# A fused delta-rule attention and MLP kernel: a new hand-written order for steps two to four, the substitution and the weight conversions of its opening

## Chip, cores and metric

The kernel runs on one core of one Trainium2 chip. The metric is device microseconds (us) for the whole kernel, lower being better. Before the change the median of three runs is 663.7 us (661.84 to 664.44).

## What is computed

The first half is a recurrent delta rule over 768 tokens, for 4 batches and 8 heads of width 48. The second half is an MLP with a hardswish on the 3072 rows that result.

```python
def _attn_ref(q, k, v, beta):
    k_n = k / (np.linalg.norm(k, axis=-1, keepdims=True) + 1e-06)
    for t in range(S):
        y[:, :, t] = np.einsum('bhd,bhde->bhe', q[:, :, t], state)
        v_old = np.einsum('bhde,bhd->bhe', state, kt)
        state = state + bt[:, :, :, None] * np.einsum('bhd,bhe->bhde', kt, vt - v_old)
def _moe_ref(x, w_in, w_out):          # x: 3072 x 384, d_ff 2048
    h = x @ w_in
    g = h * np.clip(h + 3.0, 0.0, 6.0) / 6.0
    return (g @ w_out).astype(np.float32)
```

The two weight matrices arrive as 64-bit floats. The kernel converts them to fp32 on the chip.

## The kernel before

**Tiling.** The tokens are cut into 24 steps of 32 tokens. One step holds all four batches (4 x 32 = 128 partitions) and all heads. Within a step the recurrence becomes a triangular system, whose inverse X is needed; across steps a state is carried. Two steps make one block of 256 rows for the MLP. The steps are grouped for the inversion: step 0 alone is group 0, steps 1 to 4 are group 1, and so on by fours.

**Order.** The instructions of each engine run in the order in which the program issues them. For steps 0 to 4 and the first MLP block that order is a text, `ORDER` (L22 to L41): each word advances one generator by one piece (`do`, L1428), and `*3` says it three times. From step 5 on a planner in the code takes over (L1469). Python generators fix only the order of issue, so every wait follows from data and buffers.

**Words that matter here**, with the number of the step or group behind the letter:

- `k`, `q`, `v`, `w`: one DMA issue on SyncE (SP) each. Keys, queries and values come in four parts per step; `w` is a 768 KB piece of weights, 16 in all (`load_w`, L320). A piece 6 or later reuses the buffer of an earlier one.
- `a`: one of four ScalarE instructions per weight piece, which build the power of two of each weight (`scales`, L345, instruction at L356). In this text a7.2 is the third of the four for piece 7, counting from zero. They write one of two buffers in turn, so a8.0 waits until the last conversion of piece 6 has read its buffer (L352).
- `c`: one of three VectorE instructions per piece, which convert the weights (`convert`, L366; L378, L383, L389). c6.2 is the last one of piece 6, and it needs a6.3.
- `n4`: norms of the keys of step 4 (`norms`, L399): a square and a root on ScalarE, the rest on VectorE.
- `p4`: preparation of step 4 (`prep`, L505), seven pieces: scaled keys on GpSimd; TensorE transposes of keys; a ScalarE copy; transposes of queries; a copy; scores on TensorE (L547); two VectorE products (L558) that mask the scores.
- `m`, `b`: the mask and the beta-scaled keys on GpSimd (L486, L498). `z` and `s`: settings.
- `x0`: the inverse of step 0 by products (`product`, L569).
- `i1`: the inverses of steps 1 to 4 together (`halves_of`, L715), 31 VectorE pieces: a transposition (L469), 28 small products and subtractions by turns (L730, L735), a memset, and a transposition back (L473). The first needs the masked scores of all four steps. It leaves the inverse of the two diagonal halves of each triangle.
- `x1`: the joining of the halves for step 1 (`join`, L666): a memset, a VectorE transposition (L694), a TensorE product (L684), a VectorE sum and transposition (L698, L702), a second product (L684), a ScalarE copy (L710).
- `h1`: the chain of step 1 (`chain`, L787): the product with the state on TensorE (L806), R on VectorE (L901, L909), the product with X (L827), its copy Z on ScalarE (L927), the product for the state (L938), the new state on VectorE (L956). Step 0 has no state yet and begins with the product with X.
- `y1`: the output of step 1 (`output`, L837), six pieces: a ScalarE copy (L843), a VectorE sum (L819), a TensorE product with Z (py, L827), a VectorE sum, the transposes (yt, L873), and a ScalarE copy into the MLP's input xT (L877). `y0` has four: py, copy, yt, copy.
- `ua`, `ra`, `ga`: one column block of the up product for step 0's rows: six matmuls (L994), the ScalarE relu (L1001), the VectorE rest (L1004). There are 16 column blocks; each pair needs one converted weight piece. `ub`, `rb`, `gb` do the same for step 1's rows.

**Buffers.** Results of TensorE go to four rotating slots (`pm`, L144) for everything named above but the scores and states, which share two (`pc`). The scores of a step free their slot when both masked products have read them; the first state product `h0` needs both slots.

The words ORDER holds just before the stretch that the change touches end in

```
n4 k p1 k p2*2 x0*2 a*2 c a*2 q*3
a*2 w v p3*2
```

so at its start step 0's inverse lacks one piece, keys of steps 2 and 3 are on their way through TensorE, weight pieces 0 to 2 are converted and the scalings of piece 3 are done.

Of the kernel before, what the change touches and what calls it, by code (L numbers as in the profile page):

```python
# [22 lines left out]
k*2 B*3 k*2 n0 k*2 z B s*2 n0*6 k*2 q*2 n1 q n1 q w k p0 z*3 k n1*2 k*2 n1*2 z p0*2 s k p0*3 a k a  # L23
m0 a n2 m1 p0 x0*2 w q x0 n1 x0*3 c*2 n2 a k s p1*2 a s*2 k q s*2 x0 n2 k*2 c x0 n2 x0 w q a*4 q p1
n2 k*2 a x0 m2 p1 c*2 p1 n2*3 b1 q b0 s p1 x0 q w x0 n2 q*2 c*3 x0 n4 k p1 k p2*2 x0*2 a*2 c a*2 q*3
a*2 w v p3*2 q x0 q n4 p2*2 c p2 v c n4*2 a*3 z v n4 c a m3 v c p2 n4*2 q p2 k c b2 h0 c h0 w a*2 h0
p4*2 a*2 m4 p3 q*4 h0 q k w p4*2 c*5 v*2 p3 k p3*3 k*2 p4*2 v*2 p4 m6 k a w a w i1*3 k i1*7 a i1*2 a
i1*2 v i1*2 k b3 k y0 c y0*3 ua*2 ra*2 i1*3 w v ga v a*3 i1*2 ua i1 h1 i1 q w ua ra ua i1 ra*2 ga i1
k ua a*2 ra ga i1 ga ua ra ua ra i1 ga i1*4 ua ga n5 x1*2 k x1 c a ra v a*2 ga x2 k*2 ga*2 ua*2 x1
ra*2 x1*2 ua h1*2 n5 k ga c ra ga*2 h1 c y1*2 ua ra w ga ua ra x2 n5 ga y1*2 ua ra ga h1 v*3 n5*2 k  # L30
y1*2 ua a ra x2 ub*2 a n5 rb*2 h1 x3 ga c*2 v W a h2 y2 gb ub rb gb x2 gb ub*2 n5*2 b4 rb n5 x2*2 h2
gb rb gb m5 a n5*2 y2 ub rb gb v c q*2 v q*5 n5 ub n5 rb gb h2 c h2 q ub y2 h2 y2 rb ub p5 b5 rb
gb*2 a*2 x3 p5 ub y2*2 k p5*2 h2 rb h3 p5 gb h3 ub*2 q rb gb rb gb ub a x3 p6 v c x4 x3 rb gb ub p7
rb gb y3 c*2 v c p7*2 y3 v p7*2 b6 x3 q x3 ub p6 h3 a p6 c p5*2 rb gb k m7 w p6 h3 u p6 k*2 q*3 a*2
y3 a p6 c y3 v y3*2 u n9 v k q a c a c*2 u*2 ru gu w k a*2 c a*2 x4 c*2 ru p7 a gu k u a*2 p7 p6 m8
u*3 a k u*2 k h3 w ru*2 a*2 gu*2 x4 c*2 x4 k c*2 a p8 k a*2 u ru k h3 u*2 h4 ru a b8 gu k gu y4 p8*3
u h4 k*2 c q k*9 q u p8*2 x4 k ru k*2 gu k c n9 q u q*2 p8 k*2 b7 n9*2 i2 u x4 q i2*2 q ub ru gu u
rb gb i2*2 h4*2 u*2 i2 ru i2*6 y4 i2 gu i2*7 u i2 ru gu i2 u*3 ru i2*4 gu ru i2*2 v i2 c gu u*3 a u
ru c i2 u*2 i2 gu i2*3 q i2*5 y4 h4 n9 i2 e*2 n9*2 i2*4 q i2 y4 e n9 u ru i2*3 u i2 ru*2 gu h4 u n9
i2*2 u i2 e i2*6 y4 u k n9*3 u gu i2 y4 n9 i2 p9 q i2*2 gu  # L40
"""  # L41


# [1521 lines left out]
```

## Time and profile before

| | |
|---|---|
| median of three runs | 663.7 us |
| the profiled execution, its own time | 662.06 us |
| its span in the profile | 660.3 us |
| PE busy, share of the span | 632.5 us, 96% |
| DVE busy | 499.2 us, 76% |
| ACT busy | 282.3 us, 43% |
| POOL busy | 225.1 us, 34% |
| matmul and weight-load instructions | 11640 each |

PE is TensorE's matmul stream, PEld its weight loads, DVE VectorE, ACT ScalarE, POOL GpSimd, SP the engine that issues most DMAs. Shares over the whole span hide the stages: in the first 50 us PE is busy for little more than half of the time, later all the time. So the views used below are those of stretches of time: a table of busy time by stretch, the chain of work that ended last, and the instructions in order of time. Times in them are us from the span's start. The busy time of PE is modelled, and a busy PE is not PE at its peak. The granted clock (PEclk) is the share of full speed that TensorE was allowed.

### The profile page before, as it was taken

What the parts mean: (1) busy time and instruction counts of PE and PEld (TensorE: products, weight loads), DVE (VectorE), ACT (ScalarE), POOL (GpSimd) and SP (SyncE); (2) the same over time, 40 slices, a digit from 0 to 9 for tenths busy, and PEclk for the clock granted to TensorE, in tenths of its full rate; (3) what the DMA queues carried; (4) which work ended last, traced back from release to release, by engine and by line L of the source; (5) the groups of instructions that cost most, each with busy time, mean ns of one, the idle gap of its engine ahead of it and who ended that gap; (6) DMA issues with size and microseconds to landing.
All of it is one profiled execution on the core that took longest, in us unless ns stands there. A gap on an engine that the chain in (4) does not pass through costs nothing.

```text
span 660.3 us, 26640 instructions
## 1 busy us (share of the span) xinstructions
PE 632.5 (96%) x11640; PEld 569.2 (86%) x11640; DVE 499.2 (76%) x1170; ACT 282.3 (43%) x548; POOL 225.1 (34%) x352
## 2 busy tenths in 40 slices
PE   2768999999999999999999999999999999999997
PEld 2658987776689989999999999999999999999997
DVE  5899877798657988758988848979658998456354
ACT  5887689332243154154154244244244144153250
POOL 6531022003661353553254354164051242331430
PEclk9998999999999999999999999999999999999999
DMA  7888346202040030041030030020020020000000
GB/s 174 204 198 235 77 102 164 51 25 43 9 87 18 3 74 3 3 90 22 3 74 3 2 74 3 2 63 2 3 50 2 3 49 3 23 18 2 26 1 24
DMA packets 88692, 33.28 MB, mean 50 GB/s; under 512 B 80224, under 2 KB 83424, under 8 KB 88576
## 3 DMA queue, kind: packets, MB, share of 16 engines
q1 hardware_dynamic: 88224, 31.29, 20.8%
q8 instruction: 91, 1.49, 0.9%
q10 hardware_dynamic: 352, 0.30, 0.2%
q14 instruction: 25, 0.20, 0.1%
HBM read 26.84 MB, written 4.72 MB: 48 GB/s over the span
## 4 chain that ended last, share of the span: by engine, by line
PE 91%; DVE 3%; DMA 2%; SPq 1%; ACT 1%; issue 1%; DVEq 0%
PE po L1226 28%; PE ph L1066 27%; PE ph L994 9%; PE po L1162 6%; PE ks L806 4%; PE su L938 3%; PE pt L524 3%; PE pz L827 3%; PE py L827 3%; PE sc L547 2%; PE yt L873 1%; DMA spare<-in_moe_w_in_dram 1%; PE pi L684 1%; DMA w_out<-in_moe_w_in_dram 1%; SPq L168 1%
## 5 line engine op out<-in xcount | busy, mean ns | idle before, releaser
L1066 PE MATMUL ph<-xT,w_in 128*128 128x128 f32 (+1 forms) x720 | 156.8, 321 | 0.0
L1030 POOL TENSOR_TENSOR g<-g 128x256 f32<-128x256 f32 (+1 forms) x144 | 88.6, 616 | 104.7 <-ACT g L1080 99.1
L1066 PEld LDWEIGHTS ph<-xT,w_in 128*128 128x128 f32 x720 | 116.8, 191 | 6.7
L1226 PE MATMUL po<-w_out,g 128*128 128x192 f32 x640 | 110.6, 326 | 0.0
L1226 PEld LDWEIGHTS po<-w_out,g 128*128 128x128 f32 x640 | 104.6, 190 | 0.5
L1080 ACT ACTIVATE g<-ph 128x512 f32<-128x512 f32 x72 | 43.1, 598 | 105.1 <-PE ph L1066 105.1
L1226 PE MATMUL po<-spare,g 128*128 128x192 f32 x480 | 86.7, 332 | 0.0
L1226 PEld LDWEIGHTS po<-spare,g 128*128 128x128 f32 x480 | 77.2, 190 | 1.8
L994 PE MATMUL ph<-xT,w_in 128*128 128x128 f32 (+1 forms) x384 | 72.0, 338 | 0.6 <-ACT xT L877 0.6
L1236 POOL TENSOR_TENSOR o<-o,u 128x192 f32<-128x192 f32 x18 | 13.3, 739 | 163.8 <-ACT o L1233 86.6
L994 PEld LDWEIGHTS ph<-xT,w_in 128*128 128x128 f32 x384 | 59.6, 195 | 7.7 <-ACT xT L877 0.8
L1093 DVE TENSOR_TENSOR g<-ph,g 128x256 f32<-128x256 f32 x72 | 30.2, 419 | 46.8 <-PE ph L1066 33.5
L759 DVE TENSOR_TENSOR pr<-A 128x30 f32<-128x30 f32 (+9 forms) x150 | 57.3, 382 | 3.3
L1212 DVE TENSOR_TENSOR g<-g 128x512 f32<-128x512 f32 x80 | 56.1, 722 | 3.5 <-PE po L1226 3.5
L1113 DVE SCALAR_TENSOR_TENSOR g<-o,g 128x512 f32<-128x512 f32 x72 | 52.6, 730 | 7.8 <-ACT o L1110 7.7
L764 DVE TENSOR_TENSOR A<-A,pr 128x30 f32<-128x30 f32 (+9 forms) x150 | 55.1, 367 | 3.3
L1110 ACT ACTIVATE o<-g,halves 128x512 f32<-128x512 f32 x72 | 52.2, 725 | 11.3 <-DVE g L1113 8.4
L1066 PE MATMUL ph<-beta_tok,sums_in 128*128 128x128 f32 x288 | 55.9, 275 | 0.0
L356 ACT ACTIVATE spare<-spare,places 128x768 uint16<-128x768 uint16 (+1 forms) x56 | 52.8, 947 | 3.2 <-DMA kf<-in_k_dram 1.6
L1233 ACT ACTIVATE o<-po 128x192 f32<-128x192 f32 x40 | 13.3, 332 | 82.7 <-PE po L1226 79.2
L510 POOL TENSOR_TENSOR kb<-kf,inv 128x384 f32<-128x384 f32 x24 | 21.7, 907 | 75.5 <-issue 43.1
L1162 PE MATMUL po<-w_out,g 128*128 128x384 f32 x128 | 45.4, 490 | 0.0
(141 smaller groups left out, 1019.1 us busy)
## 6 DMA issues: line engine op xcount, KB each, us to landing
kf<-in_k_dram SPq DMA_DIRECT2D x96, 48.0 KB, 2.6
qb<-in_q_dram SPq DMA_DIRECT2D x96, 48.0 KB, 2.4
vf<-in_v_dram SPq DMA_DIRECT2D x96, 48.0 KB, 2.1
out_dram<-o SPq DMA_DIRECT2D x90, 48.0 KB, 1.6
spare<-in_moe_w_in_dram SPq DMA_DIRECT2D x4, 768.0 KB, 6.6
w_out<-in_moe_w_in_dram SPq DMA_DIRECT2D x4, 768.0 KB, 6.1
w_out<-in_moe_w_out_dram SPq DMA_DIRECT2D x4, 768.0 KB, 5.8
spare<-in_moe_w_out_dram SPq DMA_DIRECT2D x4, 768.0 KB, 5.2
```

Source lines behind the costliest of these rows:

```text
L356: nc.scalar.activation(out=z, in_=z if n else d.bitcast(I16)[:, :, :, 3], func=func, bias=places[:, n : n + 1], scale=scale,)
L759: nc.vector.tensor_tensor(out=pv, in0=A[:, j + 1 :, j].unsqueeze(2).to_broadcast([n, w, j]), in1=A[:, j, 0:j].unsqueeze(1).to_broadcast([n ...
L764: nc.vector.tensor_tensor(out=A[:, j + 1 :, 0:j], in0=A[:, j + 1 :, 0:j], in1=pv, op=ALU.subtract)
L994: nc.tensor.matmul(ph[:, cols], lhsT=w_in[:, s, f * 128 : (f + 1) * 128], rhs=xT[:, s, cols], start=(s == 0), stop=(s == NKT - 1),)
L1030: nc.gpsimd.tensor_tensor(out=out, in0=a, in1=b, op=op)
L1066: nc.tensor.matmul(ph[:, n], lhsT=w, rhs=x, start=start, stop=stop, skip_group_check=True)
L1080: nc.scalar.activation(out=gt, in_=ph[:], func=ACTF.Copy)
L1110: nc.scalar.activation(out=r, in_=g, func=ACTF.Relu, bias=half, scale=1.0 / 6.0)
L1113: nc.vector.scalar_tensor_tensor(out=g, in0=r, scalar=1.0, in1=g, op0=ALU.min, op1=ALU.mult)
L1162: nc.tensor.matmul(pos[c][:], lhsT=gs[blk, f // 2][:, f % 2, c * P : (c + 1) * P], rhs=w_out[:, f, :], start=(f == 0), stop=(f == NFC - 1),)
L1212: nc.vector.tensor_tensor(out=A(f, *out, 4), in0=A(f, *a, 4), in1=A(f, *b, 4), op=op)
L1226: nc.tensor.matmul(ps[n][:], lhsT=A(f - f % 2, *a)[:, f % 2], rhs=b[:, f], start=(f == 0), stop=(f == HF - 1),)
```

## The change

Only the text `ORDER` changes. The first 148 and the last 338 of its 782 words stay as they are. The 296 between them are the same words in another order, so that every instruction of before is there once, on the same engine and of the same shape. The core of the diff, from which the unchanged words that merely wrap differently are left out (the new stretch ends at `n5 k c` in its last line):

```diff
@@ -23,21 +23,21 @@
-a*2 w v p3*2 q x0 q n4 p2*2 c p2 v c n4*2 a*3 z v n4 c a m3 v c p2 n4*2 q p2 k c b2 h0 c h0 w a*2 h0
-p4*2 a*2 m4 p3 q*4 h0 q k w p4*2 c*5 v*2 p3 k p3*3 k*2 p4*2 v*2 p4 m6 k a w a w i1*3 k i1*7 a i1*2 a
-i1*2 v i1*2 k b3 k y0 c y0*3 ua*2 ra*2 i1*3 w v ga v a*3 i1*2 ua i1 h1 i1 q w ua ra ua i1 ra*2 ga i1
-k ua a*2 ra ga i1 ga ua ra ua ra i1 ga i1*4 ua ga n5 x1*2 k x1 c a ra v a*2 ga x2 k*2 ga*2 ua*2 x1
-ra*2 x1*2 ua h1*2 n5 k ga c ra ga*2 h1 c y1*2 ua ra w ga ua ra x2 n5 ga y1*2 ua ra ga h1 v*3 n5*2 k
...
+a*2 w v p3*2 m3 b2 q n4 x0 q p2*2 n4 c p3 v*2 p3 n4 p2 n4*3 p4 c p4 p3 p2 p4 v q*3 w c p3 a p2 m4 c
+k p4 p3 p4 h0 a c p4 q*3 k w h0 p4 i1 a v*2 k*3 h0 a y0 v*2 h0 c y0 k w y0 a y0 w m6 i1*3 ua a k
+i1*3 ra ua z i1*2 a ga ra ua v i1*2 a ga ra h1 k b3 k i1*3 ga c*2 ua ra w ua ra i1*3 ga a c v ua ra
+ga i1*3 ua ra ga a v i1*3 ua ra ga i1*3 ua ra ga a q w i1*2 ua ra ga a k i1*2 ua ra ga a i1 x1*2 x2
+x1 n5 c k x1 ua ra a h1 ga x1*2 c v k*2 a h1 c a*2 c a*3 n5 k c ga h1 c y1*2 ua ra w ga ua ra x2 n5
...
```

Spelled out, with what each engine's queue sees:

- The preparation of steps 2, 3 and 4 comes first. Norms, `p3` and `p4` are interleaved from the first word on; the scores of step 4 stand before the first state product and before step 0's output, where before `h0` was complete ahead of the scores of step 3.
- The first `i1` is issued after conversions c3.0 to c4.1 (five pieces), where before c3.0 to c6.1 (eleven) stood ahead of it. c4.2, c5.0, c5.1 and c5.2 now stand inside the substitution, and c6.0 to c7.1 behind it. Before, only c6.2 stood inside, and c7.0 and c7.1 behind.
- The new state of step 0 (`h0`, last piece) and one settings piece (`z`, nine small memsets) stand inside the substitution, where before both were ahead of it.
- Step 0's output `y0` starts behind the first `i1`, where before half of the substitution was ahead of it. Eleven of the first twelve `ua` and ten `ga` stand ahead of the last `i1`; before it were eight `ua` and five `ga`.
- The scalings a4.0 to a8.3 are spread anew. The last six, a7.2 to a8.3, stand between the last piece of `x1` and the fourth piece of `h1` (Z on ScalarE). Before, all of them were ahead of that last piece of `x1`.
- On SP the last two query parts of step 4 go ahead of weight piece 5; the other loads keep nearly their places.

More of the change, by code (lines that the diff above doesn't have):

```diff
@@ L30 @@
-ra*2 x1*2 ua h1*2 n5 k ga c ra ga*2 h1 c y1*2 ua ra w ga ua ra x2 n5 ga y1*2 ua ra ga h1 v*3 n5*2 k
[L31 to L39, printed above, removed]
@@ L40 @@
-i2*2 u i2 e i2*6 y4 u k n9*3 u gu i2 y4 n9 i2 p9 q i2*2 gu
+a*2 w v p3*2 m3 b2 q n4 x0 q p2*2 n4 c p3 v*2 p3 n4 p2 n4*3 p4 c p4 p3 p2 p4 v q*3 w c p3 a p2 m4 c
[3 more added lines that the diff above has]
+x1 n5 c k x1 ua ra a h1 ga x1*2 c v k*2 a h1 c a*2 c a*3 n5 k c ga h1 c y1*2 ua ra w ga ua ra x2 n5
@@ new lines @@
+ga y1*2 ua ra ga h1 v*3 n5*2 k y1*2 ua a ra x2 ub*2 a n5 rb*2 h1 x3 ga c*2 v W a h2 y2 gb ub rb gb
+x2 gb ub*2 n5*2 b4 rb n5 x2*2 h2 gb rb gb m5 a n5*2 y2 ub rb gb v c q*2 v q*5 n5 ub n5 rb gb h2 c h2
+q ub y2 h2 y2 rb ub p5 b5 rb gb*2 a*2 x3 p5 ub y2*2 k p5*2 h2 rb h3 p5 gb h3 ub*2 q rb gb rb gb ub a
+x3 p6 v c x4 x3 rb gb ub p7 rb gb y3 c*2 v c p7*2 y3 v p7*2 b6 x3 q x3 ub p6 h3 a p6 c p5*2 rb gb k
+m7 w p6 h3 u p6 k*2 q*3 a*2 y3 a p6 c y3 v y3*2 u n9 v k q a c a c*2 u*2 ru gu w k a*2 c a*2 x4 c*2
@@ L41 @@
+ru p7 a gu k u a*2 p7 p6 m8 u*3 a k u*2 k h3 w ru*2 a*2 gu*2 x4 c*2 x4 k c*2 a p8 k a*2 u ru k h3
+u*2 h4 ru a b8 gu k gu y4 p8*3 u h4 k*2 c q k*9 q u p8*2 x4 k ru k*2 gu k c n9 q u q*2 p8 k*2 b7
+n9*2 i2 u x4 q i2*2 q ub ru gu u rb gb i2*2 h4*2 u*2 i2 ru i2*6 y4 i2 gu i2*7 u i2 ru gu i2 u*3 ru
+i2*4 gu ru i2*2 v i2 c gu u*3 a u ru c i2 u*2 i2 gu i2*3 q i2*5 y4 h4 n9 i2 e*2 n9*2 i2*4 q i2 y4 e
+n9 u ru i2*3 u i2 ru*2 gu h4 u n9 i2*2 u i2 e i2*6 y4 u k n9*3 u gu i2 y4 n9 i2 p9 q i2*2 gu
 """
```

## Prediction

> **What bounds the kernel now.** I read the table of busy time by stretch first (us from the span's start; busy us of each engine, granted clock, DMA share, GB/s).
>
> ```profile
> core 0: us, PE busy (x) PEld busy (x) DVE busy (x) ACT busy (x) POOL busy (x), PEclk, DMA share, GB/s
> 30.00:40.00 10.00, 6.33 (x245) 5.54 (x250) 8.82 (x28) 7.71 (x11) 4.79 (x5) 1.00 0.86 192
> 40.00:50.00 10.00, 6.16 (x243) 5.29 (x235) 9.25 (x15) 9.38 (x13) 3.39 (x7) 1.00 0.80 217
> 50.00:60.00 10.00, 9.42 (x120) 8.86 (x121) 9.28 (x35) 7.08 (x13) 0.20 (x2) 0.83 0.97 274
> 60.00:70.00 10.00, 9.06 (x360) 8.15 (x359) 9.41 (x26) 7.21 (x17) 2.15 (x4) 1.00 0.40 108
> 70.00:80.00 10.00, 10.00 (x311) 9.35 (x311) 8.61 (x24) 8.32 (x19) 0.00 (x0) 1.00 0.30 89
> ```
>
> From 30 to 70 VectorE (DVE) is the full engine. From about 62 on TensorE (PE) is, and the chain of waits stays with PE to the end. So what PE loses behind the substitution is not won back, and what it gains ahead of it counts only if PE is then let through. Next, that chain around the changed stretch (start, us, what).
>
> ```profile
> 45.50 0.61 DVE spare L383
> ...
> 47.79 1.86 DVE A L469
> ...
> 58.71 2.00 DVE X L473
> ...
> 60.83 0.37 DVE sums_in L694
> 61.24 0.72 PE pi L684 x54
> ...
> 67.44 0.81 PE py L827 x64
> ```
>
> Conversions run until the substitution starts (transposition A, 47.7 in the instructions in order of time). X is back at 60.7, x1's transposition ends at 61.2, py of step 1 starts at 67.4. Py is where I compare: in both orders ua13 and ua14 stand just ahead of it, and the same words behind. Last, ScalarE (ACT) in order of time.
>
> ```profile
> 58.63 1.00 ACT L356 ACTIVATE spare<-w_out,places 128x768 uint16<-128x768 int16 x1
> ...
> 61.78 1.92 ACT L356 ACTIVATE spare<-spare,places 128x768 uint16<-128x768 uint16 x2
> ...
> 64.22 0.28 ACT L710 ACTIVATE X<-pi 128x128 f32<-128x128 f32 x1
> ...
> 65.94 0.49 ACT L927 ACTIVATE R<-pz 128x384 f32<-128x384 f32 x1 [0.51 <-PE pz L827]
> 66.33 0.58 ACT L843 ACTIVATE y<-ks,parity 128x384 f32<-128x384 f32 x1
> ```
>
> The last scalings (a8.2, a8.3) end at 63.7, before X1's copy (L710) and Z1 (L927, "R"). Z1 releases py.
>
> **Part 1: scores first.** Nothing is removed; all is moved. I follow each queue from 32, where the order begins to differ, with durations of these rows. DVE: norm sum 32.0 to 32.5, x0's last piece to 33.0; root (0.3) on ACT; c3.0 (0.55); four small norm pieces (0.2 each) to 34.4. GpSimd: m3 (1.9) and b2 (0.8) end at 33.3 as before, then keys of step 4 (0.83) to 35.5. PE: their transposes (1.1) to 36.7, scores of steps 2 and 3 (1.5 for both, row at 45.2) to 38.2, query transposes to 39.2; ACT's copy (0.6, behind a4.0, 1.0) to 39.9; scores of step 4 to 41.3; the two masked products (0.75) to 42.1. A thus starts at **42.1**, 5.6 earlier. The five conversions there (0.56, 0.96, 0.95 by turns) fit beside that chain; DVE waits some 2 us in it. On SP two 0.45 us issues of queries pass weight piece 5, which lands by some 41 (6.1 us to landing) and is first read by a5.0 at about 45; that hides them. Were it not hidden, a5.0 would be late by as much, and it stands ahead of xT0. Piece 11 can be issued only after c6.1 (59 before, some 65 now); it lands in some 5 us and its scaling comes some 30 us later, so I cost it at nothing. The value loads behind it on SP are for step 3, some 20 us off.
>
> **Part 2: what now stands inside the substitution.** From A to the end of x1's transposition before took 61.2 - 47.7 = 13.5. Added: the state update 1.0, c4.2 0.95, nine memsets 0.5, c5.0 to c5.2 2.65 (42.26 to 44.91 for such three), four more `ga` at 0.2, and waits of `ga` on relus behind scalings of 0.96 on ACT, 0.5. Taken out: c6.2, 0.9. That is 5.5, so 42.1 + 13.5 + 5.5 = **61.1**. The head start is spent: the inverse comes as before. PE meanwhile starts `ua` at 46.6 in place of 51.05 (Z0 41.3, state product 43.5, py0 44.3, copy, transposes, and a copy behind a5.0 on ACT), and does eleven in place of nine blocks by then. That is the gain, at most two blocks of 0.77, or 1.5 us of PE time, and PE needs it only if it is the one waited for.
>
> **Part 3: behind the substitution.** From 61.1: first product 61.9; c6.0 (0.55) hides in that wait; sum and transposition (0.8) to 62.75; R (1.35) to 64.1; `ga` 0.2; c6.1 (1.0); c6.2 (0.95) to **66.2**. On ACT: relu 12 to 63.15, a7.1 to 64.1, X1 64.4, a7.2, a7.3 to 66.3. Now a8.0 waits for c6.2, and then a8.0 to a8.3 run (four at 0.96 to 1.0, 3.9) to 70.2. Behind them is Z1 (0.5), to 70.7, and behind Z1 the copy of y1 and relus 13 on. Py starts at 70.75, against 67.37. PE takes ua13 at 66.3 when c6.2 gives its weights, ua14 to 67.9, and then **stands for about 2.9 us**. c7.1, `ga` 12 and c7.2 end on DVE at about 69.4, just ahead of it. The sum at py is **+3.4 us**, and as PE has no wait left behind it, the same at the end.
>
> A check from DVE alone. Before, it comes through the same pieces (to the last `ga` ahead of Z1) at 66.3, with 1.8 us of waits from 32.0 on, so 32.5 of work. In the new order c7.0, c7.1, a norm sum and a `ga` (2.25) lie behind c6.2, so c6.2 ends at 32 + 30.25 = 62.25 with no wait at all, and at 65.2 with the 2.9 that I found. Then a8.x, Z1 and a gap of 0.1 make py 66.8 (-0.6) or 69.7 (+2.4). So the terms I can bound give -0.6 to about +5 (A a us later from slower cold matmuls, conversions at the 1.3 to 1.5 us that some took beside GpSimd). I take the walk, +3.4.
>
> **The clock.** [...] After 2.41 us without a matmul, 0.55 of transposes and 0.58 more, the granted clock fell:
>
> ```profile
> 51.00:52.00 1.00, 0.95 (x7) 0.95 (x8) 0.90 (x4) 0.00 (x0) 0.00 (x0) 0.90 1.17 274
> 52.00:53.00 1.00, 1.00 (x7) 1.00 (x6) 0.90 (x4) 0.37 (x1) 0.00 (x0) 0.50 1.07 258
> 54.00:55.00 1.00, 1.00 (x21) 0.78 (x22) 0.99 (x2) 0.97 (x2) 0.00 (x0) 0.50 1.01 270
> 55.00:56.00 1.00, 1.00 (x57) 0.95 (x53) 0.91 (x4) 0.97 (x2) 0.00 (x0) 0.89 0.80 136
> ```
>
> Half clock for 0.2 + 3 + 0.2 = 3.4 us. PE could spare that there, since it waited for X afterwards. Behind py it could not: half of 3.4 is 1.7 us lost. [...]
>
> **The rivals.**
> 1. *The stop also lowers the clock*: +3.4 + 1.7 = +5.1. For it, the row above; against it, that stops of 1.7 us near 39 left the clock at 1.00.
> 2. *DVE gets through with few waits*, or later waits behind py swallow part: py at -0.6 to +2.4, middle about +1. For it, the check above; against it, that the scores' chain leaves DVE idle whatever is cheap.
> 3. *Faster*: PE's early start is what counts. It decides once Z1 is ready when ua14 ends, that is if c6.2 ends by about 62 - some 4 us before my walk - or if the six scalings do not hold Z1. Then two blocks of `ua` done early are 1.5 us gained at py, and if steps 1 to 3 behind it no longer meet conversions, the 4.45 us of the earlier `ua` is the most: -1.5 to -4.5, about 660 on the medians. The conserved DVE work speaks against it.
> 4. *The change does nothing*: not possible in the order of the queues; only its sum may be near nothing, which is rival 2.
>
> **The numbers.** Against the profiled execution's own 662.06 us (span 660.3 and 1.8 around it) the forecast is 665.5. That execution lies 1.6 below the median of the runs shown, 663.7; on the median it is 663.7 + 3.4 = **667.1**. Rival 1 gives 668.8, rival 2 about 664.7, rival 3 659 to 662. Chances: forecast 0.43 (666 to 668.2), rival 1 0.25, rival 2 0.23, rival 3 0.09. The range runs from rival 2's lower half, 663.3, to rival 1 with a late A, 670.5. It leaves out rival 3 and the ends of rival 2. Half a per cent, 3.3 us, is about what a measurement of this kernel can tell from no change. Slower by more: rival 1 and about half of the forecast's own spread, 0.47. Faster by more: rival 3 where it gains over 3.3, 0.08. Within: 0.45.
>
> **What would show it.** Right: A starts near 42, X ends near 60.7, Z1 sits behind L356 rows at about 70, PE idles 2 to 3 us ahead of py at about 70.7, then shows none. The clock row behind py tells rival 1. Wrong: Z1 before 68, X before 58, or a PE that still waits or catches up between 75 and 110; or A later than 44, with more than +5.

## The result and the profile after

The changed kernel takes 670.68 us (median of 6 runs, 669.68 to 673.97); the kernel before, run beside it, 662.97 (6 runs, 661.84 to 664.44). The ratio is 1.0126, 95% interval 1.0099 to 1.0154: slower, by 7.7 us on the medians where +3.4 was forecast, and just above the upper end of the range, 670.5. The profiled execution took 670.85 us (span 669.0), 8.8 more than that of before.

First the table of busy time by stretch of the kernel after, with the columns of the prediction's first fence.

```profile
core 0: us, PE busy (x) PEld busy (x) DVE busy (x) ACT busy (x) POOL busy (x), PEclk, DMA share, GB/s
30.00:40.00 10.00, 7.11 (x260) 6.22 (x260) 8.96 (x19) 6.82 (x11) 5.43 (x6) 1.00 0.83 184
40.00:50.00 10.00, 6.59 (x214) 5.34 (x215) 6.67 (x24) 4.88 (x7) 2.26 (x5) 0.56 0.84 233
50.00:60.00 10.00, 10.00 (x124) 9.72 (x123) 7.58 (x27) 6.41 (x15) 0.00 (x0) 0.76 0.87 224
60.00:70.00 10.00, 5.84 (x208) 5.11 (x208) 9.29 (x22) 7.19 (x12) 2.86 (x4) 0.75 0.21 38
70.00:80.00 10.00, 8.60 (x218) 7.75 (x216) 6.38 (x15) 7.03 (x14) 0.00 (x0) 0.56 0.30 92
```

VectorE, the full engine of before, lost work in every stretch from 40 on: from 30 to 70 it is busy 32.5 us against 36.8. The granted clock, 0.83 in one stretch of before, is below 0.8 in four. The trace of before is no typical one in this: its mean granted clock is 0.997, and of 60 executions of that kernel on record with a clock only four reach 0.995. The 49 below 0.99 have a median of 663.16 us, the other 11 one of 662.99, so a lower mean clock does not show in the time of that kernel. Next the chain of waits from 37 to 75.

```profile
37.64 0.59 PE pt L524 x4
38.23 0.64 PE pz L827 x48
38.87 2.47 issue
41.34 0.54 PE pz L827 x16
...
61.39 1.96 DVE X L473
63.37 0.46 DVE sums_in L694
63.87 0.76 PE pi L684 x54
...
70.19 2.92 DMA vf<-in_v_dram
73.11 0.46 ACT R L927
73.61 1.50 PE py L827 x64
```

"issue" is time in which TensorE waited for nothing that the profile shows: it stood for 2.47 us in the middle of pz0, behind its 48th record. (Such a product leaves two records in the trace: pz0 is 32 products in the program and 64 records, a `ua` three and six. This text counts records.) X comes back at 63.3 (before 60.7), x1's transposition ends at 63.82 (61.19), py of step 1 starts at 73.61 (67.37). Now VectorE in order of time, only the rows with a wait and A; the bracket is the idle time and what ended it.

```profile
43.10 0.42 DVE L558 TENSOR_TENSOR L<-sc,sums_in 128x256 f32<-128x256 f32 x1 [2.90 <-PE sc L547]
...
43.78 1.95 DVE L469 STREAM_TRANSPOSE A<-L 128x1024 f32<-128x1024 f32 x1
...
51.37 0.29 DVE L1004 SCALAR_TENSOR_TENSOR g<-g,ph 128x128 f32<-128x128 f32 x1 [1.32 <-ACT g L1001]
...
52.65 0.29 DVE L1004 SCALAR_TENSOR_TENSOR g<-g,ph 128x128 f32<-128x128 f32 x1 [0.52 <-ACT g L1001]
```

A starts at 43.78 (before 47.70), behind a wait of 2.90 us for step 4's scores. Inside the substitution VectorE waits for relus: 1.32, 0.52 and, behind a third `ga`, 0.19 us. Last, ScalarE ahead of Z1 ("R", L927) in order of time.

```profile
69.27 1.02 ACT L356 ACTIVATE spare<-w_out,places 128x768 uint16<-128x768 int16 x1 [0.37 <-DVE w_in L389]
70.31 2.87 ACT L356 ACTIVATE spare<-spare,places 128x768 uint16<-128x768 uint16 x3
73.09 0.47 ACT L927 ACTIVATE R<-pz 128x384 f32<-128x384 f32 x1
```

This is the queue that the prediction spoke of: a8.0 waits for c6.2, four scalings run, then Z1. Z1 starts at 73.09 (before 65.94; forecast 70.2). The chain above puts Z1 down to a load of values that lands at 73.11 instead. But ScalarE is busy with the scalings until then, and in e1 and e7 below Z1 starts (70.98 and 69.59) within 0.5 us of the first of these loads' issue (70.55 and 69.20), and the one such load of the kernel after whose landing is known took 5.3 us. So Z1 does not wait for the load.

TensorE in order of time shows what it loses: before, then after.

```profile
51.05 3.55 PE L994 MATMUL ph<-xT,w_in 128*128 128x128 f32 x18 [0.58 <-ACT xT L877]
...
65.83 1.60 PE L994 MATMUL ph<-xT,w_in 128*128 128x128 f32 x12
...
73.20 1.15 PE L806 MATMUL ks<-state,KQ 64*64 64x48 f32 x64
```

```profile
49.29 4.21 PE L994 MATMUL ph<-xT,w_in 128*128 128x128 f32 x18 [0.58 <-ACT xT L877]
...
63.87 0.73 PE L684 MATMUL pi<-X,sums_in 16*32 16x16 f32 x64 [3.11 <-DVE sums_in L694]
...
69.28 2.93 PE L994 MATMUL ph<-xT,w_in 128*128 128x128 f32 x12 [0.58 <-DVE w_in L389]
73.61 1.50 PE L827 MATMUL py<-R,LB 32*32 32x48 f32 x64 [1.40 <-ACT R L927]
...
81.56 1.15 PE L806 MATMUL ks<-state,KQ 64*64 64x48 f32 x64
```

The last rows of both are the milestone still needed: the next state product, `ks` of step 2, starts at 81.56 (before 73.20). From there to the end it takes 587.4 us against 587.1. So all that counts is lost by then, 8.36 us, and it divides at two points:

| from, to | before | after | difference | forecast |
|---|---|---|---|---|
| start to the end of x1's transposition | 61.19 | 63.82 | +2.63 | -0.1 |
| to py | 6.18 | 9.79 | +3.61 | 3.4 to 3.5 |
| to ks of step 2 | 5.83 | 7.95 | +2.12 | 0 (rival 1: +1.7) |

### The profile page after: what moved, and what is told of

The parts are those of the page before. It is cut to its first block, busy times and chain, and to the rows that moved or that the text cites. A ratio compares the mean times of both kernels' runs of the same rounds, so it can differ in the third digit from the quotient of the medians.

```text
span 669.0 us, 26639 instructions
## 1 busy us (share of the span) xinstructions
PE 638.1 (95%) x11640; PEld 573.8 (86%) x11640; DVE 499.7 (75%) x1170; ACT 281.5 (42%) x548; POOL 224.8 (34%) x352
## 3 DMA queue, kind: packets, MB, share of 16 engines
q8 instruction: 91, 1.49, 0.9%
## 4 chain that ended last, share of the span: by engine, by line
PE 91%; DVE 3%; SPq 2%; DMA 2%; issue 1%; ACT 0%; POOL 0%; DVEq 0%; POOLq 0%
PE po L1226 28%; PE ph L1066 27%; PE ph L994 9%; PE po L1162 6%; PE ks L806 4%; PE py L827 3%; PE su L938 3%; PE pz L827 3%; PE pt L524 3%; PE sc L547 3%; PE yt L873 1%; SPq L168 1%; DMA spare<-in_moe_w_in_dram 1%; DMA w_out<-in_moe_w_in_dram 1%; PE pi L684 1%
## 5 line engine op out<-in xcount | busy, mean ns | idle before, releaser
L1066 PE MATMUL ph<-xT,w_in 128*128 128x128 f32 (+1 forms) x720 | 156.9, 321 | 0.1
L1066 PEld LDWEIGHTS ph<-xT,w_in 128*128 128x128 f32 x720 | 116.8, 191 | 6.7
L994 PE MATMUL ph<-xT,w_in 128*128 128x128 f32 (+1 forms) x384 | 74.9, 348 | 1.3 <-DVE w_in L389 0.6
L994 PEld LDWEIGHTS ph<-xT,w_in 128*128 128x128 f32 x384 | 62.3, 205 | 9.0 <-ACT xT L877 1.0
```

Source lines behind the costliest of these rows:

```text
L994: nc.tensor.matmul(ph[:, cols], lhsT=w_in[:, s, f * 128 : (f + 1) * 128], rhs=xT[:, s, cols], start=(s == 0), stop=(s == NKT - 1),)
L1066: nc.tensor.matmul(ph[:, n], lhsT=w, rhs=x, start=start, stop=stop, skip_group_check=True)
```

## The experiments

**Theory Q**: the scalings ahead of Z1 hold py, and a stop of TensorE lowers the clock. **Rival I**: the loss is the late inverse. Later, **theory F**: TensorE runs out of instructions at fixed places of its own stream. Distances: "X" is the start of the transposition back (L473), and X-py and py-ks run to the starts of py and of ks of step 2. The interval is that of the ratio to the kernel before on the same chip, whose median lies between 662.61 and 663.69 us.

| kernel | X | X-py | py-ks | median, us | ratio, 95% |
|---|---|---|---|---|---|
| before | 58.71 | 8.66 | 5.83 | 662.97 | |
| after | 61.39 | 12.22 | 7.95 | 670.68 | 1.0099 to 1.0154 |
| e1 | 63.51 | 10.75 | 8.29 | 673.22 | 1.0135 to 1.0184 |
| e2 | 57.87 | 12.71 | 7.21 | 668.08 | 1.0053 to 1.0091 |
| e3 | 61.98 | 8.68 | 5.83 | 666.58 | 1.0038 to 1.0082 |
| e4 | 60.93 | 12.50 | 7.38 | 669.88 | 1.0073 to 1.0131 |
| e5 | 63.65 | 13.71 | 5.83 | 680.95 | 1.0227 to 1.0275 |
| e6 | 61.16 | 12.54 | 5.83 | 670.11 | 1.0062 to 1.0118 |
| e7 | 62.17 | 10.74 | 7.22 | 670.37 | 1.0072 to 1.0113 |
| e8 | 61.76 | 8.74 | 7.11 | 666.98 | 1.0036 to 1.0071 |

### e2: the late scalings alone, in the kernel before

```diff
-ga v a*3 i1*2 ua i1 h1 i1 q w ua ra ua i1 ra*2 ga i1 k ua a*2 ra ga i1 ga ua ra ua ra i1 ga i1*4 ua
+ga v a*2 i1*2 ua i1 h1 i1 q w ua ra ua i1 ra*2 ga i1 k ua ra ga i1 ga ua ra ua ra i1 ga i1*4 ua
-ga n5 x1*2 k x1 c a ra v a*2 ga x2 k*2 ga*2 ua*2 x1 ra*2 x1*2 ua h1*2 n5 k ga c ra ga*2 h1 c y1*2
+ga n5 x1*2 k x1 c ra v ga x2 k*2 ga*2 ua*2 x1 ra*2 x1*2 ua h1*2 n5 k ga c ra ga*2 a*6 h1 c y1*2
```

All six, a7.2 to a8.3, go just ahead of Z1.

> The order of before, with one edit: the six scalings a7.2 to a8.3 stand just ahead of Z1 of step 1. Theory Q: ScalarE reaches them at 65.4, Z1 at about 71.2, py at 71.8 in place of 67.4 (+4.4), and a stop of some 4 us lowers the clock for 3.4 us or more (+1.7 to 2), total 667.4 to 669.5. Rival I: the inverse is as early as before, so at most 1 us slower, 663 to 664.

Measured 668.08 us, as Q expected. Its ScalarE rows and its py, from the instructions in order of time:

```profile
67.28 2.87 ACT L356 ACTIVATE spare<-spare,places 128x768 uint16<-128x768 uint16 x3
70.06 0.47 ACT L927 ACTIVATE R<-pz 128x384 f32<-128x384 f32 x1
```

```profile
70.58 0.88 PE L827 MATMUL py<-R,LB 32*32 32x48 f32 x64 [4.07 <-ACT R L927]
```

The inverse was 0.8 us *earlier* than before (X at 57.87), and yet py came 3.2 later, behind a stop of 4.07 us that ends with Z1; then half clock came (0.50 from 72 to 74; the stretches of 1 us to either side have 0.71 and 0.59) and py-ks grew by 1.4. The scalings in front of Z1 are a cause by themselves, worth 4 us from X to py.

### e3 and e4: the change in two halves

e3 has the order of after up to the first `i1` (the scores first) and the remaining words as before has them; e4 the reverse. Where they leave the kernel after (e3) and the kernel before (e4):

```diff
-h0 p4 i1 a v*2 k*3 h0 a y0
+h0 p4 i1 a z a c a*2 h0 a*2 h0
```

```diff
-w a w i1*3 k i1*7 a
+w a w i1 y0*4 i1*3 ua k
```

> The changed order up to the first piece of the substitution, and from there the remaining words in the order of before: scores first alone. Theory Q: the substitution starts near 43.8, the conversions that before stood ahead of it stand just behind its first transposition, scalings are early, so 663 to 665. Rival I: scores first itself is the loss (the stop of 2.5 us in the first product with X, the half clock from 41 to 55), so 666 to 669.

> The order of before up to the first piece of the substitution, and from there the remaining words in the changed order. Theory Q: the substitution starts at 47.7 and ends near 61, c6.2 near 66, then the four scalings of piece 8, Z1 at 70 to 71, py 3 to 4 us late, and the clock: 666 to 669. Rival I: inverse on time, so 663 to 665.

e3: 666.58, between the two kernels, inside Rival I's range and above Q's. Its A starts at 44.17 and its X at 61.98, 3.3 later than before; X-py and py-ks are those of before to 0.02 us. So moving the scores ahead is a loss of its own, and Rival I holds for that part. TensorE stood 2.85 us in pz0, and VectorE was busy 0.72 of the 4 us from 40 to 44. e4: 669.88, just above what Q expected: X is 2.2 late and X-py 3.8 longer. The halves cost 3.6 and 6.9 by the medians, together more than the whole (7.7): each makes X late, by 3.3 and 2.2 us, and in the changed kernel X is late by 2.7 and not by their sum.

### e1 and e7: take the scalings away from Z1

In e1 the four of piece 8 go behind relu 14, in e7 one each behind relus 13, 14, 15 and behind the last piece of y1.

```diff
-a h1 c a*2 c a*3 n5 k c ga h1 c y1*2 ua ra w ga ua ra x2
+a h1 c a c n5 k c ga h1 c y1*2 ua ra w ga ua ra a*4 x2
```

```diff
-a h1 c a*2 c a*3 n5 k c ga h1 c y1*2 ua ra w ga ua ra x2
+a h1 c a c n5 k c ga h1 c y1*2 ua ra a w ga ua ra a x2
...
```

> The changed order, with the four scalings of piece 8 moved behind the relu of ua14, so that Z1 of step 1 no longer stands behind them on ScalarE. Theory Q (the queue ahead of Z1 holds py, and the stop lowers the clock): Z1 at about 69 in place of 73.1, py right behind ua14 at 71 to 72.2 in place of 73.6, total 1.5 to 3 us under the changed order, 667.7 to 669.2. Rival I (the inverse that comes 2.6 us late, and the work inside the substitution, are the loss; the scalings only fill a wait): within 0.7 us of the changed order, 670 to 671.4.

> The changed order, with the four scalings of piece 8 taken out of the way of Z1 one at a time: behind the relus of ua13, ua14 and ua15, and behind the copy into xT. Theory Q: Z1 about 5.5 us behind X in place of 9.8, py at once behind ua14 (8.8 behind X in place of 10.3), xT not held, so 1.5 to 3 us less from X to the next product with the state (18.2 in the changed order), total 668 to 669.5. Rival I (late inverse): X to that product as in the changed order within 0.7.

Both brought X-py down by 1.5 us, as Q said, and neither made the kernel faster. e1 missed by 4 us: 2.1 us were lost ahead of X (A came 0.4 later, and a stop in the state product su0 was 1.99 us where the kernel after has 0.24), and the four scalings, now ahead of step 1's copy into xT, let it start only at 80.49. e7's gain was 2.2 us from x1's transposition to ks, and 0.3 us by the median: 0.8 was lost ahead of X, and 1.4 was lost again behind ks. So of the 3.6 us from X to py only 1.5 come back with those four words: then py stands right behind ua13 and ua14, which wait for c6.2 and run at half clock (2.93 us for the two in both runs, where the kernel before took 1.60). That the rest returns behind ks because VectorE and ScalarE still have the work to do is argued.

### e5: keep the clock up

14 unread 128x128 products of the identity ahead of x1's first product, 8 ahead of py's piece (`D` counts them).

```diff
+        elif word[0] == "D":
+            warm(int(word[1:]))
...
-i1 x1*2 x2 x1 n5 c k
+i1 x1*2 x2 D14 x1 n5 c k
...
-x2 n5 ga y1*2 ua ra
+x2 n5 ga D8 y1*2 ua ra
```

> The changed order, with 22 matmuls whose result nothing reads: 14 of them just ahead of x1's first product, where TensorE stood for 3.1 us, and 8 just ahead of py of step 1, where it stood for 1.4. Theory Q with the clock as a term of its own: the granted clock stays at 1.00 from 60 to 80, the stretch from py to the next product with the state shrinks from 7.95 to about 5.9 us, and the blocks ahead of py by about 1, so 2 to 3 us under the changed order, 667.7 to 668.7. Rival (the half clock there only fills waits for VectorE and ScalarE): within 0.7 us of the changed order.

680.95 us, a bad miss, and the clock fell all the same, from 69.8 to 76.7. What it shows: with the clock back at 1.00 behind py, py-ks is 5.83 us, that of before.

```profile
77.36 0.88 PE L827 MATMUL py<-R,LB 32*32 32x48 f32 x64
...
83.19 1.15 PE L806 MATMUL ks<-state,KQ 64*64 64x48 f32 x64
```

But the products ran 3.39 and 3.04 us, and the eight held py for 1.4 us behind Z1. X was 2.3 us later than in the kernel after, behind a stop of 3.95 us in pz0, and TensorE showed new "issue" stops far behind the edit, among them 1.70 us at 94 and 2.59 at 113. From ks to the end it took 596.6 us instead of 587.4. These stops led to the form of theory F that e9 tests.

### e6 and e8: hold a weight load, to shorten the stop in pz0

The load of piece 6 waits until step 4's scores are through (`W`); e6 is the kernel after with it, e8 is e3 with it.

```diff
-q*3 k w h0 p4 i1
+q*3 k W h0 p4 i1
```

> The changed order, with the load of weight piece 6 held on SyncE until the scores of step 4 are done on TensorE. Theory F (the 2.5 us stop inside the first product with X, at which no engine waits for anything the profile shows, is TensorE out of instructions, whose blocks are fetched late beside two 768 KB weight loads): the stop shrinks to under 1 us, the substitution starts near 42, the half clock from 41 to 55 is gone or shorter, total 2 to 4 us under the changed order, 667 to 669. Rival (the stop has another cause, or the fetch is slow by itself): the stop stays at 2 us or more, and the total within 1 us of the changed order.

> Scores first alone (the changed order up to the first piece of the substitution, then the words of before), with the load of weight piece 6 held as in the other kernel of this set. Theory F: the stop inside the first product with X is gone, the substitution starts near 42 in place of 44.2, total 662 to 664.5, against 666.6 with the stop. Rival: 666 to 667.5, as without the hold.

670.11 and 666.98: no gain. The stops in pz0 were 1.66 and 2.67 us and A started at 43.74 and 43.55, so this load is not what makes the stop. e6 says one thing more: its clock came back at 72.9 instead of 78.7, py-ks was 5.83, ks came 2.0 earlier than in the kernel after, and the whole was only 0.6 faster by the medians (1.3 by the profiled spans). Of the 2.1 us behind py, then, not all is shown to reach the end. Nor is half clock all that can lengthen that stretch: e8 has full clock there, two stops of 0.48 and 0.41 us, and 7.11.

### e9 to e16: the same shift of TensorE's stream in both kernels

Unread products of two 16x16 corners of the identity ahead of everything, where TensorE is idle until 8.2 us (with 20 of them its first transposition starts at 7.99). Their number is the only difference: 16, 20, 31 or 63, in the kernel after and in the kernel before.

```diff
-q w k p0 z*3
+q w k D20 p0 z*3
```

> The changed kernel with 20 products of two 16x16 corners of the identity put on TensorE before its first transposition, where it is idle until 8.2 us; nothing reads them. Theory F (TensorE runs out of instructions at fixed places of its own stream, about 126 products apart, and stands until the next block is there): the stop after the 48th product of pz0 moves to the 28th and that after the 46th of su0 to the 26th, each of any size up to 4 us; the time stays within 668 to 673 us, since a stop in the same stretch remains. Rival P (the stop belongs to the moment, 38.9 us, or to what else is in flight then, not to the place in the stream): the stop stays at about 38.9 us, after the 48th product of pz0 or wherever TensorE then is, and the time within 1 us of 670.7.

> The kernel before with the same 20 products before its first transposition. Theory F: its two stops move from the 62nd score product of step 2 to about the 42nd and from the 61st product of su0 to about the 41st, and stops can come up where there was none, so the time may rise: 663 to 668 us. Rival P: stops and time as before, 662.5 to 663.7 us.

> The changed kernel with 63 such products, half a block. Theory F: no stop within pz0 or su0; instead one near the 117th of the 128 score products ahead of pz0 (at about 37.4 us) and one near the 47th of the 64 score products behind pz0. If the stop at pz0 is part of the loss because it falls on the path to the substitution, the substitution starts within 0.8 us of 42.1 and the time falls to 667 to 670 us; if the stop merely moves with its full size, 670 to 672 us. Rival P: the stop stays at 38.9 us and the time within 1 us of 670.7.

> The kernel before with 63 such products. Theory F: the two stops of before move to the transpositions ahead of step 2's scores and to the end of pz0 (about its 62nd product); with the stretch from 26 to 43 us as busy on TensorE as in the kernel after they may be as long as there, which gives 664 to 668 us; if they stay below 1 us, 662.5 to 664 us. Rival P: stops and time as before, 662.5 to 663.7 us.

> The changed kernel with 31 unread products of two 16x16 corners ahead of everything, half a block by the count that the shifts of 20 and 63 gave (such a product takes the room of two). Theory F with Q (the place of the blocks sets which stops there are, and the order costs its 4 us or more besides): the stop leaves pz0 for the end of the 128 score products ahead of it and the one in su0 for the 64 score products behind pz0; the time is 4 to 11 us above that of the kernel before with the same shift. Theory F alone (the difference of the two kernels is mostly the place of the blocks): within 2 us of it, or below it.

> The kernel before with the same 31 products. Both theories: its stops move to the first score product of step 2 and to the end of pz0, and it has others later; between 663 and 677 us. The two differ on its distance to the changed kernel with the same shift: 4 to 11 us for F with Q, under 2 us or the other way for F alone.

> The changed kernel with 16 such products, a quarter of a block. Stops near the 16th product of pz0 and the 14th of su0. F with Q: 4 to 11 us above the kernel before with the same shift. F alone: within 2 us of it, or below it.

> The kernel before with the same 16 products. Stops near the 30th score product of step 2 and the 29th product of su0, others later; between 663 and 677 us. F with Q: 4 to 11 us below the changed kernel with the same shift. F alone: within 2 us of it, or above it.

| added | before, us (ratio) | after, us (ratio) | difference, us |
|---|---|---|---|
| 0 | 662.97 | 670.68 (1.0126) | 7.7 |
| 16 | 674.81 (1.0187) | 682.47 (1.0306) | 7.7 |
| 20 | 675.29 (1.0194) | 683.26 (1.0306) | 8.0 |
| 31 | 672.98 (1.0152) | 681.07 (1.0262) | 8.1 |
| 63 | 663.88 (1.0013) | 672.63 (1.0147) | 8.8 |

The 95% intervals of these ratios reach 0.002 to 0.003 to either side, those of after with 31 and 16 products 0.006 and 0.004.

The place of the stops does follow the stream. In the kernel after, 20 products moved the stop in pz0 from behind the 48th record to behind the 8th, 16 to behind the 16th; 63 put it behind the 50th, nearly where it was. (Each of the added products counts for two, and F's 28th was wrong by that; 63 of them are a whole block.) So the stops recur every 126 records or so. The places forecast for 16 and 31 products are in the traces too, except for the kernel before with 31. And the place matters far more than either theory allowed for (F gave at 20 products at most 668 us before and 673 after), though hardly between the two kernels. These are three of the ten stops of the kernel *before* with 20 products added, from TensorE's instructions in order of time:

```profile
40.93 0.98 PE L938 MATMUL su<-R,sums_in 32*64 32x48 f32 x43 [2.42 <-issue]
...
54.20 3.14 PE L994 MATMUL ph<-xT,w_in 128*128 128x128 f32 x13 [1.62 <-issue]
...
108.14 0.46 PE L547 MATMUL sc<-KQ 64*32 64x64 f32 x31 [3.10 <-issue]
```

They add up to 12.4 us, and that kernel is 12.3 slower than before; unshifted, its stops sum to 0.75 in the order-of-time view. The two kernels keep their distance of 7.7 to 8.8 at every place, which rules out F alone: the order is the cause, not the luck of where its stops fall. The traces of the five pairs say what repeats. X to py takes 8.6 to 9.1 us in the kernels before and 12.2 to 12.5 in those after; X is 2.7 to 6.5 us late; and the stops of the kernel after sum to 1.6 to 2.3 us more than those of its pair. So some 2 of the 8 us go with stops that this order meets wherever its blocks lie.

The traces also show what lands ahead of such a stop. The profile's DMA table has a queue of the kind "instruction" (q8) with 91 packets and 1.49 MB, 16.4 KB each, and the packed trace has the time of each. The order-of-time views of the kernels after and before show three stops at "issue" on TensorE, and they end 1.31, 1.45 and 1.50 us behind the landing of such a packet: in the kernel after one lands at 40.03 and the stop in pz0 ends at 41.34; it is the fifth, and in the kernel before the fifth lands at 39.81 and the one stop ends at 41.31. The 11640 matmul records over 91 packets are an estimated 128 to a packet, near the 126 from stop to stop. So I read the stops as waits for the next packet. No run here changed the packets, and why one lands when it does stays open.

### e19 and e20: keep the clock with whole blocks

126 products of the small kind, two whole blocks, in the stop ahead of x1; e20 with e7's order besides.

```diff
-i1 x1*2 x2 x1 n5 c k
+i1 x1*2 x2 D126 x1 n5 c k
```

> The changed kernel with 126 products of two 16x16 corners of the identity, two whole blocks, in the stop in which TensorE waits for x1's transposition (60.8 to 63.9 us); nothing reads them. Theory C (2.1 us of the loss is the half clock behind py, which the stop of 3.1 us sets off): the stop shrinks below 1.5 us, the granted clock from 65 to 78 us is at 0.9 or more, and from py to the next chunk's first state product it takes 5.8 to 6.2 us instead of 7.95; the time is 667.7 to 669.3 us. Rival G (that stretch is bound by ScalarE and VectorE, and the lower clock costs nothing that counts): the clock rises, and the time stays within 0.7 us of 670.7. Where the added blocks are themselves fetched late, x1 starts later than 63.9 us, and the comparison goes by the distances behind it.

> The same 126 products in the kernel with piece 8's scalings spread behind four relus (370.4 - 1.0 is its x1 and 670.37 us its time). Theory C with Q: the queue's 2.2 us and the clock's 2.1 us both come off the stretch from x1's transposition to the next chunk's first state product, which falls from 18.2 us to 14 to 14.8; the time is 666 to 668.5 us. Rival G: that stretch stays at about 16 us and the time at 669.7 to 671 us.

(The "370.4 - 1.0" in the second text is a slip and means nothing.) 675.62 us (ratio 1.0158 to 1.0213) and 673.96 (1.0150 to 1.0198), both missed, and neither theory is decided by it, for the clock fell all the same. In e19, a row of TensorE in order of time and the table by stretches of 1 us:

```profile
62.93 6.64 PE L1436 MATMUL wm<-ident 16*16 16x16 f32 x251
```

```profile
66.00:67.00 1.00, 1.00 (x47) 1.00 (x44) 0.50 (x2) 0.00 (x0) 0.00 (x0) 1.00 0.00 0
67.00:68.00 1.00, 1.00 (x42) 1.00 (x39) 0.00 (x0) 0.00 (x0) 0.00 (x0) 0.50 0.00 0
```

TensorE was busy without a gap from 62.9 to 69.6, and was put to half clock at 67. They also ran twice as long as the stop they were to fill, so x1 started at 69.4.

## Why the prediction missed

The direction was right, and so was the one mechanism that the forecast rests on; but that is 3.6 of the 8.4 us. The size failed in three terms.

1. **The queue ahead of Z1: right.** From x1's transposition to py the forecast was 9.65 us (61.1 to 70.75); the trace has 9.79, and to Z1's start 9.27 against 9.1. e2 shows the cause alone. One step inside was off: TensorE was to stand for 2.9 us ahead of py and stood for 1.40, since ua13 and ua14 ran at half clock and took 2.93 us, not 1.60. So without the scalings py could come only some 1.4 us earlier, which is what e1 and e7 found (1.5).
2. **"A thus starts at 42.1": 1.68 too early.** The walk ahead of A summed instructions, and TensorE stood 2.47 us in pz0 at "issue", with step 4's scores queued behind. No row of before had such a stop above 0.75, and I took none. Until then TensorE was ahead of the walk (step 4's query transposes ended at 38.2, forecast 39.2), so 1.0 early and 2.47 late leave 1.5 of the 1.68. The packet ahead of the stop's end lands at 40.03, and at 39.81 in the kernel before, where TensorE got to that place at 40.56 and not at 38.87: as I read it, the new order moved work ahead of its instructions. That A would come earlier by the stop is argued; no run took it away (e6 left 1.66 of it, and its A came at 43.74).
3. **"waits of `ga` on relus ... 0.5": they were 2.03.** The `ua` whose relus they wait for began at 49.29, where 46.6 was forecast, and ran at half clock (below): 18 of their records took 4.21 us, where at full clock 12 took 1.60 (row at 80.02). The row of before (18 in 3.55 us, at 51.05, mostly at half clock too) could have told the second; there, no `ga` stood in the substitution so early. Which of the two makes the waits was not tested. So A to the end of x1's transposition took 20.04 us and not 19.0.

   Terms 2 and 3 are the +2.63 at that transposition. VectorE's own account closes on it: from 32 to there it was idle 6.89 us against 2.60 before, +4.29, and had 1.66 us less work done. The prediction's check used this account, but with 2.9 us of waits as far as c6.2, where 7.5 came (gaps between instructions included; before, it read 1.8 where the same count gives 2.7); so c6.2 ended at 69.2 and not 65.2.
4. **"PE has no wait left behind it, the same at the end": 2.12 us more to ks**, which is rival 1 (priced 1.7) in its effect, though not by its stop: the clock fell at 65.1, well ahead of the stop in front of py, so rival 1's price came near by luck. The prediction held against it that stops of 1.7 us near 39 had left the clock at 1.00; no run shows that one of 2.9 us does. (Nor is that 1.00 sure: the 64 records of pz0 took 1.50 us at 36.03 in the trace of before, as long as the 64 of py at half clock in the kernel after; at full clock those took 0.88.) In the kernel after half clock came at 41.2, just ahead of the end of a stop of 2.47 us (38.87 to 41.34), and at 65.1, 1.2 us behind the end of one of 3.11 (60.76 to 63.87). The second is no accident of this trace. Nine traces have a stop of 2.9 to 3.1 us there (after, e1, e4, e6, e7, e9, e11, e13, e15), and in each the clock falls between 1.0 us ahead of its end and 1.2 behind it; seven have one of 0.9 to 1.2 us (before, e3, e8, e10, e12, e14, e16), and in none is the clock below 1.00 between 60 and 85. These are the first and last stretches of 1 us that show it fall or return:

```profile
41.00:42.00 1.00, 0.66 (x32) 0.54 (x40) 0.00 (x0) 0.05 (x1) 0.00 (x0) 0.59 1.15 296
...
54.00:55.00 1.00, 1.00 (x52) 1.00 (x48) 0.96 (x3) 0.00 (x0) 0.00 (x0) 0.59 1.00 238
...
65.00:66.00 1.00, 1.00 (x32) 0.78 (x34) 0.95 (x3) 0.25 (x1) 0.44 (x2) 0.53 0.08 16
...
78.00:79.00 1.00, 1.00 (x7) 1.00 (x7) 0.48 (x2) 0.76 (x2) 0.00 (x0) 0.64 0.00 0
```

   The mean of such a row places the edge within it: half clock from 41.2 to 54.8 and from 65.1 to 78.7, 13.6 us each time, where the trace of before had 3.4. e5 and e6 show that at full clock the 2.12 us go; e6 shows that not all of them need reach the end. Half clock ahead of the inverse costs the order of before little: e12 has 23.9 us of it, from 33 to 57, and took 663.58.

The sum at ks is 3.4 + 1.68 + 1.04 + 0.14 + 2.12 = 8.4, against 8.36 measured. The prediction's remark that "the head start is spent" was right and too mild: `ua` started early, ran out of work 3.1 us ahead of the inverse, and a stop as long as that in front of x1 went with half clock in all nine traces that have one. Rivals 2 and 3 are out, since py was 6.24 late. "A later than 44, with more than +5" was named as a sign of error; A came at 43.8, and the sum was more than +5. The loads were priced right: no wait for a weight piece stands ahead of A. No version here beats the kernel before; the nearest is the kernel before with 63 products added (1.0013, 0.9997 to 1.0029).

What stays open: which part of 1.68 the stop in pz0 is, why its packet lands when it does (the stop varies from 1.66 to 3.95 us at one and the same place in after, e1, e3 and e5 to e8), and how much of the half clock behind py reaches the end.

## What to carry to other kernels

When a reordering pulls an engine's work forward, look at where that engine then runs out of it: here the up products came early, the inverse they had to wait for came later, and half clock came with the stop, as in all nine traces with a stop of 2.9 to 3.1 us there. Look also whether the instructions themselves are there: TensorE stood in pz0 until 1.31 us behind the landing of an instruction packet, at 40.03, no earlier than in the kernel before (39.81). Work that stands ahead of a short instruction in a queue (Z1 behind four scalings) can cost its full length as soon as the data is late (e2: 4.05 us from X to py), and is read off best by trying that one move alone. Before a difference of 1 or 2% between two orders is put down to the orders, shift both by the same few unread instructions: here such a shift moved either kernel by up to 12.6 us, and only the distance between them held.

## What the runs showed of the hardware

- TensorE's stops at "issue" recur every 126 records of small products or so (from the 48th of pz0 to the 46th of su0 in the kernel after), and the three in the traces of after and before end 1.31 to 1.50 us behind the landing of a 16.4 KB packet of the instruction queue. Over all runs they last 0.2 to 5.3 us (5.33 in the kernel before with 31 products added, ahead of the last 14 records of py0); 16 to 31 tiny products ahead of everything made the kernel before 10 to 12 us slower, 63 of them 0.9.
- Being busy does not keep the clock: under 6.64 us of 16x16 products without a gap it fell to 0.50, 4.1 us after the first of them. With e5's 14 products of 128x128 in the same place it stayed at 1.00 until 69.8.
- The stretches of half clock measured here are near multiples of 3.4 us: 3.4 before and in e2 (71.4 to 74.8), 6.8 in e5 (69.8 to 76.7), 13.6 twice in the kernel after, with 10.2 at full clock between the two, 17.1 in e3 (40.9 to 58.0) and 23.9 in e12. A stop of 2.41 us in the kernel before went with one such period and one of 2.47 in the kernel after with four; what decides is not shown.
